# Retention and a squared-ReLU layer: flipping q and k two chunks ahead, with ScalarE's copies spread over a visit

## The chip, the cores and the metric

The kernel runs on one core of a Trainium2 chip. The metric is the device time of one execution in microseconds (us). The core's engines are TensorE (PE; its weight loads are listed as PEld), VectorE (DVE), ScalarE (ACT), GpSimd (POOL) and SyncE (SP), which here only issues transfers. Each works through its own queue of instructions in order, and they wait for each other by semaphores. SBUF is the on-chip memory of 128 partitions, PSUM the accumulators that matmuls write into.

## What is computed

```python
# q, k, v: (8 batches, 8 heads, 576 positions, 64), float32
scores = scale * np.matmul(q, k.transpose(0, 1, 3, 2))
Dmat = np.where(rel >= 0, gamma[:, None, None] ** rel[None, :, :], 0.0)   # decay by distance, causal
ret = np.matmul(scores * Dmat[None], v)
x = ret.transpose(0, 2, 1, 3).reshape(4608, 512)
h = np.maximum(x @ w_in, 0.0)          # w_in (512, 2048)
out = (h * h @ w_out).astype(np.float32)  # w_out (2048, 512)
```

The two weights come in double precision; the kernel turns them into float32 on the core. All matmuls are float32.

## The kernel before

The retention is done chunk by chunk: each batch's 576 positions are four chunks of 128 and one of 64, 40 chunks in all. The decay is split into a factor on q and one on v, so that a chunk needs only a causal mask; what earlier chunks contribute comes from a running 64x64 state per head (`u`). The first product (x @ w_in) follows in blocks of 512 tokens, by a Strassen-like scheme of seven products per tile, one product per "step"; its result goes to DRAM. The second product (L893) is a phase of its own behind all this.

One pass of the main loop is called a visit here. Visit i works on the retention of chunk i-1, makes the scores of chunk i, and does matmul steps of the first product (`ffn`) in two halves, as many as a schedule of tokens asks for: typically three or four per half, but one or two in the first half behind a chunk of 64.

From chunk 9 on, q and k are transposed on VectorE in 32x32 blocks (`flip`), and ScalarE puts the blocks where they belong with 16 small copies (8 for a chunk of 64), which are queued in `moves`:

```python
def scale_q(i, engine):                      # q times its decay factor
    ...
    engine.tensor_tensor(t, t, dv[...].to_broadcast([cs, H, D]), op=ALU.mult)              # L373

def new_qk(i):
    t = work2.tile([128, 2, HP, C], F32, tag="qk", name="qk")                              # two buffers
    ...
def flip(i):
    t = st[i]["flip"] = work2.tile([128, 4, 2, HP, 32], F32, tag="flip", name="flip")
    for j in (1, 0):                                                                        # k, then q
        nc.vector.transpose(t[:cs, :, j, :, :], loaded[i][j][:cs].rearrange(...))          # L390

def spread(i):
    to = new_qk(i)
    for b in range(chunks[i][3] // 32):
        for g in range(4):
            moves.append(lambda b=b, g=g: nc.scalar.copy(                                  # L396
                to[32 * g:32 * g + 32, :, :, 32 * b:32 * b + 32], st[i]["flip"][32 * b:32 * b + 32, g, :, :, :]))

def scores(i):
    ... nc.tensor.matmul(sc[e][rows(h), hp, :], lhsT=kT[...], rhs=qT[...], ...)            # L433, sc_ps
    ... nc.vector.tensor_tensor(r[:cs], both[:cs], msk[...], op=ALU.mult)                  # L441, mask; r lies in kT
    ... nc.gpsimd.tensor_tensor(vs[:cs], vs[:cs], dv[...], op=ALU.mult)                    # L443, decay of v

def retain_a(i):   # second half of the chunk with itself, state grows; nothing for a chunk of 64
    ... matmuls L455 (x_ps) and L458 (u_ps);  nc.scalar.copy(u_sb[...], u_ps[0])           # L464

def retain_b(i):   # what the state contributes
    ... nc.tensor.matmul(x_at(hp, b, h), lhsT=u[...], rhs=s["qT"][...], ...)               # L490, x_ps
    nc.scalar.copy(u_sb[...][:, 0:2, 0:1], xp[0][:, :, cs - CH:cs - CH + 1])               # L493, two numbers a row

def retain_c(i):   # first half of the chunk with itself (L455, L458), then
    ... nc.scalar.copy(xT[n][...], p[...])                                                  # L512
```

A step of the first product and its evacuation (`ffn_in`): eight matmul records of one tile (L614, h_a, h_b or h_c), then by the product's number

```python
if j == 0:   nc.scalar.copy(p1, p)                                  # L624, needed before product 3
elif j == 1: nc.vector.tensor_tensor(u2, p, p1, op=ALU.add)         # L626
elif j == 2: nc.vector.tensor_tensor(p15, p, p1, op=ALU.add)        # L628
elif j == 3: nc.scalar.activation(g["A11"], p, AF.Relu); ...        # L630, and a square on GpSimd, L631
elif j == 4: ... # L633, and a square on VectorE, L621
elif j == 5: ... # L637, L621
else:        ... # L640, L621
# then VectorE's sums of g (L552 to L555), of x (L538 to L541), and one piece of the
# conversion of w_out: L207, L211 and L215/L216 on ScalarE, L219, L222, L225, L242 to L245
```

The loop from chunk 5 on:

```python
def move(count):
    for f in moves[:count]:
        f()
    del moves[:count]
# ffn(i, half): for each of its steps: move(3); step()

else:
    ...
    if i + 1 < N_CH:
        scale_q(i + 1, nc.gpsimd)
    retain_a(i - 1)
    if i < N_TURN:                 # N_TURN = 9: chunks 0 to 8 are transposed on TensorE
        turn(i)
    ffn(i - 1, 0)
    move(len(moves))
    if N_TURN <= i + 1 < N_CH:
        flip(i + 1)
    retain_b(i - 1)
    if i < N_CH:
        scores(i)
    retain_c(i - 1)
    if N_TURN <= i + 1 < N_CH:
        spread(i + 1)
    ffn(i - 1, 1)
...
if i + 3 < N_CH:
    load(i + 3)                    # q, k and v of chunk i + 3
```

Of the kernel before, what the change touches and what calls it, by code (L numbers as in the profile page):

```python
# [9 lines left out]
F32 = mybir.dt.float32  # L10
# [5 lines left out]
C = 128  # L16
# [24 lines left out]
def kernel(  # L41
# [33 lines left out]
    nc = tc.nc  # L75
    ctx.enter_context(tc.manual_schedule())

    B, H, S, D = q.shape
    HP = H // 2
# [12 lines left out]
    N_CH = len(chunks)  # L92
# [6 lines left out]
    only = first.enter_context(tc.tile_pool(name="only", bufs=1))  # L99
    ld3 = first.enter_context(tc.tile_pool(name="ld3", bufs=3))  # L100
    ld4 = first.enter_context(tc.tile_pool(name="ld4", bufs=4))
    work = first.enter_context(tc.tile_pool(name="work", bufs=1))
    work2 = first.enter_context(tc.tile_pool(name="work2", bufs=2))
    ps_x = first.enter_context(tc.tile_pool(name="ps_x", bufs=1, space=PS))
    ps_t = first.enter_context(tc.tile_pool(name="ps_t", bufs=1, space=PS))
# [22 lines left out]
    loaded = {}  # L128
    N_EARLY = TOK // C

    def load(i):
        b, ci, c0, cs = chunks[i]
        got = {name: pool.tile([128, H, D], F32, tag=name, name=f"{name}_ld") for name, pool in (("q", ld3), ("k", ld4), ("v", ld4))}
        if i == 0:
            nc.sync.dma_start(dv, decays)
        for name, src in (("q", q), ("k", k), ("v", v)):
            t = got[name]

            issue = nc.scalar if i == 0 and name != "q" else nc.sync
            at = src[b, :, c0:c0 + cs, :].rearrange("h s d -> s h d")  # L140
            if name == "v":
                issue.dma_start(t[:cs], at)
            else:

                issue.dma_start(t[:cs, 0:H // 2, :], at[:, 0:H // 2, :])
                for e in range(2):
                    issue.dma_start(t[:cs, H // 2 + e::2, :], at[:, H // 2 + 1 - e::2, :])
        loaded[i] = [got["q"], got["k"], got["v"]]

# [166 lines left out]
    dv = only.tile([128, H, 2 * NCH], F32, name="dv")  # L318
    exp_bias = const.tile([128, 1], F32, name="exp_bias")
    nc.gpsimd.memset(exp_bias, -896.0 * 2.0 ** 23)  # L320
    idle = only.tile([128, 128], F32, name="idle")
    nc.vector.memset(idle, 1.0)
    load(0)
    load(1)
    fetch_raw(1)
    load(2)

    ident = only.tile([128, 128], F32, name="ident")
    make_identity(nc, ident)

    msk = only.tile([128, 1, 1, CH], F32, name="msk")
# [38 lines left out]
    def scale_q(i, engine):  # L370
        ci, cs = chunks[i][1], chunks[i][3]
        t = loaded[i][0][:cs]
        engine.tensor_tensor(t, t, dv[:cs, :, NCH + ci:NCH + ci + 1].to_broadcast([cs, H, D]), op=ALU.mult)  # L373
# [5 lines left out]
    moves = []  # L379

    def new_qk(i):
        t = work2.tile([128, 2, HP, C], F32, tag="qk", name="qk")
        st[i]["qT"], st[i]["kT"] = t[:, 0, :, :], t[:, 1, :, :]
        return t

    def flip(i):
        cs = chunks[i][3]
        t = st[i]["flip"] = work2.tile([128, 4, 2, HP, 32], F32, tag="flip", name="flip")
        for j in (1, 0):
            nc.vector.transpose(t[:cs, :, j, :, :], loaded[i][j][:cs].rearrange("s (p e) (d a) -> s (e d) p a", e=2, d=2))  # L390

    def spread(i):
        to = new_qk(i)
        for b in range(chunks[i][3] // 32):
            for g in range(4):
                moves.append(lambda b=b, g=g: nc.scalar.copy(  # L396
                    to[32 * g:32 * g + 32, :, :, 32 * b:32 * b + 32], st[i]["flip"][32 * b:32 * b + 32, g, :, :, :]))

    def move(count):
        for f in moves[:count]:  # L400
            f()
        del moves[:count]

    def turn(i):

        cs = chunks[i][3]
        n_h = cs // CH
        p = ps_t.tile([128, 2, 512], F32, tag="t", name="t_ps").rearrange("p h (j d t) -> p h j d t", j=2, d=HP)
        for j in (1, 0):
            for hp in range(HP):  # L410
                for h in range(n_h):
                    nc.tensor.transpose(p[:, h, j, hp, :], loaded[i][j][rows(h), 2 * hp:2 * hp + 2, :],
                                        ident[rows(h), rows(h)])
        to = new_qk(i)[:, :, :, :cs].rearrange("p j d (h t) -> p j d h t", h=n_h)
        nc.scalar.copy(to[:, 1].rearrange("p d h t -> p h d t"), p[:, :n_h, 1, :, :])
        nc.vector.tensor_copy(to[:, 0].rearrange("p d h t -> p h d t"), p[:, :n_h, 0, :, :])
# [78 lines left out]
    def retain_c(i):  # L495

        b_, ci, c0, cs = chunks[i]
        own, grow = within(i, 0)
        more = ci + 1 < NCH
        for j in range(0, len(own), 2):  # L500
            for f in own[j:j + 2] + (grow[j:j + 2] if more else []):
                f()
        tok = b_ * S + c0
        at = tok
        p = xp[0][:, :, 0:256].rearrange("p a (g t) -> p a g t", g=2)
        while at < tok + cs:
            n = at // TOK

            while steps and steps[0][0] <= (n - 2 if n > 4 else n - 3):
                step()  # L510
            end = min(tok + cs, (n + 1) * TOK)
            nc.scalar.copy(xT[n][:, :, at - n * TOK:end - n * TOK].rearrange("p (a g) t -> p a g t", a=2),  # L512
                           p[:, :, :, at - tok:end - tok])
            if more and at == tok:
                grown(i, 1)
            at = end
            if n_next[0] < N_BLK and (n_next[0] + 1) * TOK <= at:
                steps.extend(block_steps(n_next[0]))
                n_next[0] += 1
        st[i] = loaded[i] = None  # L520
# [175 lines left out]
    def ffn(i, half):  # L696

        gone[0] += chunks[max(0, min(i, N_CH - 1))][3] / 2
        if steps and steps[0][0] == 0:

            move(6)
            for f in (step, lambda: convert(6)) if half else (lambda: convert(6), step):
                f()
            if half and steps and steps[0][0] == 0:
                step()
                convert(6)
            return
        if not behind:
            behind.append((gone[0] - HALF, done[0]))
        points = behind + [p for p in PACE if p[0] > behind[0][0]]  # L710
        want = points[-1][1]
        for (x0, y0), (x1, y1) in zip(points, points[1:]):
            if gone[0] < x1:
                want = y0 + (y1 - y0) * (gone[0] - x0) / (x1 - x0)
                break
        count = max(1, int(want) - done[0])
        while steps and count:
            held[0] = half == 0 and count == 1
            move(3)
            step()  # L720
            count -= 1
        held[0] = False
# [15 lines left out]
    for i in range(N_CH + 1):  # L738
        if i <= N_EARLY:

            if i == 1:
                convert(2)
            elif i == 2:
                convert(5)
            if i >= 1:
                retain_a(i - 1)
                if i < 3:
                    warm(4, False)
                else:
                    convert(1)  # L750
                    first_in(2 * i - 5, (0,))
                    convert(5)
                retain_b(i - 1)
                if i < 3:
                    warm(4, False)
                retain_c(i - 1)
            convert((0, 1, 1, 0, 1)[i])
            if i == N_EARLY:
                fetch_raw(2)
                step()  # L760
            scores(i)
            if i == 2:
                convert(5)
                first_in(0, (0,))
            elif i == 3:
                convert(1)
                first_in(2, (0,))
                convert(5)
            elif i == N_EARLY:
                convert(5)  # L770
                step()
                convert(6)
            scale_q(i + 1, nc.gpsimd)
            if i < N_EARLY:
                if i < 2:
                    warm(6, False)
                turn(i + 1)
        else:
            if i == N_EARLY + 1:
                gone[0] = TOK  # L780
            if i + 1 < N_CH:
                scale_q(i + 1, nc.gpsimd)
            retain_a(i - 1)
            if i < N_TURN:
                turn(i)
            ffn(i - 1, 0)
            move(len(moves))
            if N_TURN <= i + 1 < N_CH:
                flip(i + 1)
            retain_b(i - 1)  # L790
            if i < N_CH:
                scores(i)
            retain_c(i - 1)
            if N_TURN <= i + 1 < N_CH:
                spread(i + 1)
            ffn(i - 1, 1)
        if i == 0:
            fetch_raw(2)
        if i + 3 < N_CH:
            load(i + 3)  # L800
        if 0 < i < N_EARLY:
            fetch_raw(1)
    assert n_next[0] == N_BLK
# [232 lines left out]
```

## Time and profile before

The kernel took 1007.21 us (median of three runs, 1002.46 to 1008.52); the profiled execution has a span of 1007.7 us.

| | busy us | share of the span |
|---|---|---|
| PE | 966.5 | 96% |
| PEld | 861.4 | 85% |
| DVE | 786.1 | 78% |
| ACT | 351.3 | 35% |
| POOL | 128.7 | 13% |

| operation | times | mean ns |
|---|---|---|
| flip of k, of q (L390, VectorE) | 31 each | 699, 664 (medians) |
| copy into qk (L396, ScalarE) | 440 | 402 |
| scale of q (L373, GpSimd) | 39 | 1210 |
| scores (L433, TensorE) | 1152 | 233 |
| matmuls of the first product (L614, h_b) | 736 | 387 |

How to read it: a busy share is an average over the whole span. The retention and the first product end at about 605 us, the rest is the second product. A line such as "PE sc_ps L433 <- ACT qk L396: 16.1, 19, 3.6" says that TensorE's matmuls of line 433 stood idle for 16.1 us in all, in 19 waits of at most 3.6 us, until ScalarE's instruction of line 396 released them. A group's line has its busy time and mean duration, then the idle time of the engine before it and what ended most of that. In a timeline a line has its start, its length, engine, line, operation, tiles and how many instructions were merged. Matmuls are pipelined, and their ends are modelled. The granted clock is the share of TensorE's full clock that the chip let through.

### The profile page before, as it was taken

The numbers are of one execution on the slowest core, as the hardware profiler recorded it, in microseconds if no ns is written. First come the engines' busy times: TensorE is split into PE (matmuls) and PEld (weight loads), VectorE is DVE, ScalarE is ACT, GpSimd is POOL, SyncE is SP. The second block draws the span as 40 slices with busy tenths as digits, with TensorE's granted clock in tenths as the row PEclk, the third lists the DMA queues.
The fourth block names the chain that finished last, engine by engine and source line by source line (L and its number), as shares of the span: only waits on it lengthen the run. The fifth ranks groups of instructions, "written<-read, shape, count | busy, mean of one in ns | idle before, by whom it ended". The sixth has DMA issues, their size and how long they took to land. (4 is left out here: it accounts for less than half of the span.)

```text
span 1007.7 us, 24117 instructions
## 1 busy us (share of the span) xinstructions
PE 966.5 (96%) x10092; PEld 861.4 (85%) x10092; DVE 786.1 (78%) x1458; ACT 351.3 (35%) x871; POOL 128.7 (13%) x121
## 2 busy tenths in 40 slices
PE   7899989999999899989989999999999999999998
PEld 6645768788878778877878889999999999999998
DVE  3789787768998799998977677777777677777766
ACT  3454575674665656746562110000000000000000
POOL 3211212312123131212120000000000000000000
PEclk7999999999999899999989999999999999999999
DMA  8883657655798589669437998684865757565351
GB/s 196 239 226 115 171 163 208 180 154 178 204 296 236 147 247 268 211 180 297 135 126 299 394 419 320 250 293 144 287 210 187 272 176 255 187 241 209 127 210 43
DMA packets 185037, 219.19 MB, mean 218 GB/s; under 512 B 118624, under 2 KB 135008, under 8 KB 175968
## 3 DMA queue, kind: packets, MB, share of 16 engines
q1 hardware_dynamic: 182816, 217.13, 66.3%
q8 instruction: 79, 1.29, 0.5%
q10 hardware_dynamic: 2112, 0.52, 0.2%
q14 instruction: 30, 0.25, 0.1%
HBM read 128.23 MB, written 89.39 MB: 216 GB/s over the span
## 5 line engine op out<-in xcount | busy, mean ns | idle before, releaser
L396 ACT COPY qk<-flip 32x256 f32<-32x256 f32 x440 | 177.1, 402 | 34.2 <-DVE flip L390 27.8
L614 PE MATMUL h_b<-room,w 128*128 128x256 f32 x736 | 179.4, 387 | 1.9 <-DVE room L539 1.6
L614 PEld LDWEIGHTS h_b<-room,w 128*128 128x128 f32 x736 | 139.6, 193 | 23.3 <-issue 2.1
L893 PE MATMUL o_b<-w,room 128*128 128x128 f32 x1168 | 144.5, 275 | 1.5 <-DVE room L844 1.5
L893 PEld LDWEIGHTS o_b<-w,room 128*128 128x128 f32 x1168 | 137.2, 192 | 1.7 <-DVE room L844 1.7
L893 PE MATMUL o_c<-w,room 128*128 128x128 f32 x1008 | 123.0, 275 | 0.0
L893 PEld LDWEIGHTS o_c<-w,room 128*128 128x128 f32 x1008 | 117.7, 192 | 0.0
L614 PE MATMUL h_c<-room,w 128*128 128x256 f32 x480 | 116.6, 386 | 0.0
L614 PE MATMUL h_a<-room,w 128*128 128x256 f32 x448 | 109.8, 389 | 3.1 <-ACT room L624 3.1
L907 ACT COPY r<-o_a 128x128 f32<-128x128 f32 x53 | 14.1, 265 | 273.3 <-PE o_a L893 242.5
L614 PEld LDWEIGHTS h_c<-room,w 128*128 128x128 f32 x480 | 91.8, 193 | 13.2
L614 PEld LDWEIGHTS h_a<-room,w 128*128 128x128 f32 x448 | 84.9, 193 | 15.7 <-ACT room L624 3.5
L893 PE MATMUL o_a<-w,a 128*128 128x128 f32 x688 | 85.6, 275 | 0.0
L631 POOL TENSOR_TENSOR room<-room 128x512 f32<-128x512 f32 x32 | 35.4, 1105 | 387.9 <-ACT room L630 368.5
L893 PEld LDWEIGHTS o_a<-w,a 128*128 128x128 f32 x688 | 81.2, 192 | 0.1
L621 DVE SCALAR_TENSOR_TENSOR room<-room 128x512 f32<-128x512 f32 x96 | 75.5, 786 | 3.3
L578 PE MATMUL h_ps<-room,w 128*128 128x512 f32 (+1 forms) x160 | 58.7, 515 | 3.5 <-DVE w L225 2.6
L373 POOL TENSOR_TENSOR q_ld<-q_ld,dv 128x512 f32<-128x512 f32 (+1 forms) x39 | 47.2, 1210 | 76.5 <-DMA q_ld<-in_q_dram 70.1
L455 PEld LDWEIGHTS x_ps<-qk,v_ld 64*64 64x64 f32 x1152 | 42.0, 141 | 15.3 <-issue 13.7
L433 PE MATMUL sc_ps<-qk 64*64 64x64 f32 x1152 | 35.5, 233 | 19.5 <-ACT qk L396 16.1
L455 PE MATMUL x_ps<-qk,v_ld 64*64 64x64 f32 x1152 | 51.1, 230 | 3.0 <-DVE qk L441 2.0
L633 DVE TENSOR_TENSOR room<-h_b,room 128x512 f32<-128x512 f32 x32 | 22.1, 690 | 39.0 <-PE h_b L614 38.9
(111 smaller groups left out, 1419.8 us busy)
## 6 DMA issues: line engine op xcount, KB each, us to landing
g_dram<-room SPq DMA_DIRECT2D x32, 1792.0 KB, 7.8
a<-g_dram SPq DMA_DIRECT2D x43, 1024.0 KB, 7.3
room<-g_dram SPq DMA_DIRECT2D x20, 1024.0 KB, 6.3
w<-w_dram SPq DMA_DIRECT2D x7, 1792.0 KB, 12.9
out_dram<-room SPq DMA_DIRECT2D x17, 512.0 KB, 3.3
w<-in_moe_w_in_dram SPq DMA_DIRECT2D x16, 512.0 KB, 5.7
w<-in_moe_w_out_dram SPq DMA_DIRECT2D x16, 512.0 KB, 3.8
v_ld<-in_v_dram SPq DMA_DIRECT2D x31, 256.0 KB, 4.0
```

Source lines behind the costliest of these rows:

```text
L373: engine.tensor_tensor(t, t, dv[:cs, :, NCH + ci:NCH + ci + 1].to_broadcast([cs, H, D]), op=ALU.mult)
L396: moves.append(lambda b=b, g=g: nc.scalar.copy(to[32 * g:32 * g + 32, :, :, 32 * b:32 * b + 32], st[i]["flip"][32 * b:32 * b + 32, g, :, : ...
L433: nc.tensor.matmul(sc[e][rows(h), hp, :], lhsT=kT[rows(e), hp, t], rhs=qT[rows(e), hp, t], start=True, stop=True, skip_group_check=True)
L455: own.append(lambda hp=hp, e=e, b=b: nc.tensor.matmul(x_at(hp, b, h), lhsT=s["vs"][rows(h), 2 * hp + b, :], rhs=s["ret"][rows(h), e, hp, : ...
L578: nc.tensor.matmul(p.rearrange("p h t -> p (h t)"), lhsT=w[:, c, :], rhs=xT[0][:, c, lo * HT:hi * HT], start=(c == 0), stop=(c == N_DM - 1))
L614: nc.tensor.matmul(p[:, mm, :], lhsT=w[:, c, :], rhs=xs[n][right][:, c, :], start=(j in OPENS and mm == 0 and c == 0), stop=(j in CLOSES a ...
L621: nc.vector.scalar_tensor_tensor(t, t, 0.0, t, op0=ALU.max, op1=ALU.mult)
L631: nc.gpsimd.tensor_tensor(g["A11"], g["A11"], g["A11"], op=ALU.mult)
L633: nc.vector.tensor_tensor(g["A22"], p, p15, op=ALU.add)
L893: nc.tensor.matmul(p, lhsT=s["lefts"][left][:, m, :], rhs=w_out[j][:, m, WO_SLOT[right], :], start=(i in OPENS and m == 0), stop=(i in CLO ...
L907: nc.scalar.copy(r[:, 0, 0:128], p)
```

## The change

q and k are loaded one chunk further ahead (v is not), with five buffers for k. q is scaled by GpSimd behind the scores, two chunks ahead, and both are flipped at the end of a visit, two chunks ahead. The copies of a chunk into its qk tile are queued with the flip, so that they spread over all steps of the next visit, three before each step; what is left of them when their own chunk's visit begins is done behind retain_a, before its first step. Since the qk tiles of three chunks are then alive, they have three buffers. Two small constant tiles move into a part of a weight's room that is free in this phase, which makes space. The purpose is that the scores of a chunk find their operands ready.

```diff
--- before.py
+++ after.py
@@ -99,7 +99,9 @@
     only = first.enter_context(tc.tile_pool(name="only", bufs=1))
     ld3 = first.enter_context(tc.tile_pool(name="ld3", bufs=3))
     ld4 = first.enter_context(tc.tile_pool(name="ld4", bufs=4))
+    ld5 = first.enter_context(tc.tile_pool(name="ld5", bufs=5))
     work = first.enter_context(tc.tile_pool(name="work", bufs=1))
+    work3 = first.enter_context(tc.tile_pool(name="work3", bufs=3))
     work2 = first.enter_context(tc.tile_pool(name="work2", bufs=2))
     ps_x = first.enter_context(tc.tile_pool(name="ps_x", bufs=1, space=PS))
     ps_t = first.enter_context(tc.tile_pool(name="ps_t", bufs=1, space=PS))
@@ -128,13 +130,15 @@
     loaded = {}
     N_EARLY = TOK // C
 
-    def load(i):
+    def load(i, names="qkv"):
         b, ci, c0, cs = chunks[i]
-        got = {name: pool.tile([128, H, D], F32, tag=name, name=f"{name}_ld") for name, pool in (("q", ld3), ("k", ld4), ("v", ld4))}
         if i == 0:
             nc.sync.dma_start(dv, decays)
-        for name, src in (("q", q), ("k", k), ("v", v)):
-            t = got[name]
+        got = loaded.setdefault(i, [None] * 3)
+        for name, pool, src in (("q", ld3, q), ("k", ld5, k), ("v", ld4, v)):
+            if name not in names:
+                continue
+            t = got["qkv".index(name)] = pool.tile([128, H, D], F32, tag=name, name=f"{name}_ld")
 
             issue = nc.scalar if i == 0 and name != "q" else nc.sync
             at = src[b, :, c0:c0 + cs, :].rearrange("h s d -> s h d")
@@ -145,7 +149,6 @@
                 issue.dma_start(t[:cs, 0:H // 2, :], at[:, 0:H // 2, :])
                 for e in range(2):
                     issue.dma_start(t[:cs, H // 2 + e::2, :], at[:, H // 2 + 1 - e::2, :])
-        loaded[i] = [got["q"], got["k"], got["v"]]
 
 
 
@@ -318,14 +321,13 @@
     dv = only.tile([128, H, 2 * NCH], F32, name="dv")
     exp_bias = const.tile([128, 1], F32, name="exp_bias")
     nc.gpsimd.memset(exp_bias, -896.0 * 2.0 ** 23)
-    idle = only.tile([128, 128], F32, name="idle")
+    idle, ident = (W[6][:, at:at + 128] for at in (2688, 2816))
     nc.vector.memset(idle, 1.0)
     load(0)
     load(1)
     fetch_raw(1)
     load(2)
 
-    ident = only.tile([128, 128], F32, name="ident")
     make_identity(nc, ident)
 
     msk = only.tile([128, 1, 1, CH], F32, name="msk")
@@ -379,7 +381,7 @@
     moves = []
 
     def new_qk(i):
-        t = work2.tile([128, 2, HP, C], F32, tag="qk", name="qk")
+        t = work3.tile([128, 2, HP, C], F32, tag="qk", name="qk")
         st[i]["qT"], st[i]["kT"] = t[:, 0, :, :], t[:, 1, :, :]
         return t
 
@@ -389,17 +391,16 @@
         for j in (1, 0):
             nc.vector.transpose(t[:cs, :, j, :, :], loaded[i][j][:cs].rearrange("s (p e) (d a) -> s (e d) p a", e=2, d=2))
 
-    def spread(i):
         to = new_qk(i)
-        for b in range(chunks[i][3] // 32):
+        for b in range(cs // 32):
             for g in range(4):
-                moves.append(lambda b=b, g=g: nc.scalar.copy(
-                    to[32 * g:32 * g + 32, :, :, 32 * b:32 * b + 32], st[i]["flip"][32 * b:32 * b + 32, g, :, :, :]))
-
-    def move(count):
-        for f in moves[:count]:
-            f()
-        del moves[:count]
+                moves.append((i, to[32 * g:32 * g + 32, :, :, 32 * b:32 * b + 32], t[32 * b:32 * b + 32, g, :, :, :]))
+
+    def move(count, i=N_CH):
+
+        while moves and count and moves[0][0] <= i:
+            nc.scalar.copy(*moves.pop(0)[1:])
+            count -= 1
 
     def turn(i):
 
@@ -778,26 +779,31 @@
         else:
             if i == N_EARLY + 1:
                 gone[0] = TOK
-            if i + 1 < N_CH:
-                scale_q(i + 1, nc.gpsimd)
             retain_a(i - 1)
             if i < N_TURN:
                 turn(i)
+            move(C, i)
             ffn(i - 1, 0)
-            move(len(moves))
-            if N_TURN <= i + 1 < N_CH:
-                flip(i + 1)
             retain_b(i - 1)
             if i < N_CH:
                 scores(i)
+            for j in range(i + 1 + (i > N_EARLY + 1), min(i + 3, N_CH)):
+                scale_q(j, nc.gpsimd)
             retain_c(i - 1)
-            if N_TURN <= i + 1 < N_CH:
-                spread(i + 1)
             ffn(i - 1, 1)
+            if N_TURN <= i + 2 < N_CH:
+                flip(i + 2)
         if i == 0:
             fetch_raw(2)
-        if i + 3 < N_CH:
+        if i < N_TURN - 1:
             load(i + 3)
+        else:
+            if i == N_TURN - 1:
+                load(i + 3, "qk")
+            if i + 4 < N_CH:
+                load(i + 4, "qk")
+            if i + 3 < N_CH:
+                load(i + 3, "v")
         if 0 < i < N_EARLY:
             fetch_raw(1)
     assert n_next[0] == N_BLK
```

## The prediction

> **What bounds the kernel now.** I read the windows first (busy time by stretch), then the waits of the first 560 us, then the timeline around single waits. After about 605 us only the second matrix product runs: TensorE is busy for 354.35 of the last 357 us, and the change touches nothing there. So everything has to be decided between 95 us (first flip) and 560 us. The columns are stretch, length, then busy time of PE, PEld, DVE, ACT, POOL, granted clock, DMA share, GB/s:
>
> ```profile
> 100.00:250.00 150.00, 143.41 (x1714) 118.89 (x1713) 116.33 (x178) 89.90 (x219) 36.97 (x32) 0.99 0.62 178
> 250.00:345.00 95.00, 89.56 (x1009) 75.56 (x1010) 83.81 (x137) 62.17 (x148) 21.12 (x19) 0.96 0.77 225
> 345.00:440.00 95.00, 89.50 (x1082) 75.10 (x1074) 90.14 (x143) 59.60 (x144) 20.86 (x18) 0.99 0.70 209
> 440.00:560.00 120.00, 113.51 (x1206) 96.28 (x1201) 96.09 (x157) 57.29 (x137) 23.28 (x21) 0.95 0.70 229
> ```
>
> TensorE bounds all four, but it is idle for 24.0 of 460 us (6.6 + 5.4 + 5.5 + 6.5), and VectorE is close behind it: 90.14 of 95 us in the third. The waits from 95 to 560 us say what ends the idle time (sum, times, longest):
>
> ```profile
> ACT qk L396 <- DVE flip L390: 27.8, 15, 5.7
> ...
> PE sc_ps L433 <- ACT qk L396: 16.1, 19, 3.6
> ...
> PE h_a L614 <- ACT room L624: 3.1, 1, 3.1
> ...
> PE x_ps L455 <- DVE qk L441: 2.0, 1, 2.0
> ```
>
> The scores wait for ScalarE's copies out of the flipped tile (16.1 us), and those had waited for VectorE's flips (27.8 us). The single wait of h_a has the same root: ScalarE's queue stood before a flip. The page gives the size of the copies:
>
> ```profile
> L396 ACT COPY qk<-flip 32x256 f32<-32x256 f32 x440 | 177.1, 402 | 34.2 <-DVE flip L390 27.8
> ```
>
> One such wait, in the timeline:
>
> ```profile
> 325.85 4.15 ACT L396 COPY qk<-flip 32x256 f32<-32x256 f32 x10
> ...
> 329.22 0.47 PE L433 MATMUL sc_ps<-qk 64*64 64x64 f32 x2 [2.17 <-ACT qk L396]
> ...
> 330.02 0.16 ACT L493 COPY u_sb<-x_ps 128x2 f32<-128x2 f32 x1
> ```
>
> Ten copies stand in a row because the first half-visit had only one matmul step to put them beside. The tiny copy L493 reads x_ps, which was finished at 326.79, and runs only behind the ten copies. It matters below: the next matmuls into x_ps (L455, retain_c) wait for L493, and in the timeline they start right after it wherever it comes late (330.19 and, after the last scores, 330.76 here).
>
> An idle TensorE costs twice. In the answer for 328.8 to 335.6 us the granted clock is
>
> ```profile
> 328.80:335.60 6.80, 6.02 (x53) 4.99 (x54) 5.30 (x8) 2.93 (x9) 0.58 (x1) 0.50 0.13 21
> ```
>
> and the eight h_a matmuls at 331.76 take 3.78 us instead of 1.89. In windows of 5 us there are five such dips after 100 us (at 135-145, 325-340, 435-445, 475-480 and 505-515), each after 2.1 us or more of idle time. Five times the sum of the missing clock is 12 us; about 1 us of it is idle anyway, so some 11 us are lost to slow matmuls.
>
> [...]
>
> **The change part by part.** Loads: q and k four chunks ahead. From 200 to 560 us GpSimd waited only 4.6 us for q, and the matmuls for no load at all; worth nothing by itself, it only makes the rest legal. Scaling: one 1.06 us operation moves a half-visit and a chunk; GpSimd is busy 13%, worth 0. Flips: the same 62 (0.70 and 0.66 us), moved from before retain_b to the very end of the visit, a chunk earlier. The mask product L441 thus no longer stands behind 1.37 us of flips, which should take about 1.4 of the 2.0 us that x_ps waited. Copies: the same 440 of 0.41 us, now three before each step of the whole following visit, and any rest right after retain_a. The scores of a chunk then find their copies done at least half a visit earlier.
>
> Removed idle time: 16.1 + 3.1 + 1.4 = 20.6 us. With the 11 us of clock the most that can be gained is 31.6 us, which would make 976 us.
>
> Added: the flips now come right before the copies that need them. ScalarE's first copy in a visit stops its queue until VectorE has worked off what it is behind and flipped. Before, that stop lay behind retain_c, with a whole visit until the next thing that TensorE needed of the queue's end. Now L493 comes half a visit after it. How far VectorE is behind at a visit's end can be read off. Start of retain_a and last VectorE operation of the steps before it:
>
> ```profile
> 311.62 0.27 PE L455 MATMUL x_ps<-qk,v_ld 64*64 64x64 f32 x2
> ...
> 312.29 0.68 DVE L640 TENSOR_TENSOR room<-h_b,room 128x512 f32<-128x512 f32 x1
> ...
> 314.21 0.68 DVE L222 TENSOR_TENSOR w<-w,w 128x512 f32<-128x512 f32 x1
> ```
>
> L222 ends at 314.89, 3.3 us after TensorE went on. Flips there end at 3.3 + 1.37 = 4.6. Then ScalarE has nine copies (3.7) for the three steps of this half, L624 (0.6) and L493 (0.16): done 9.1 us after the start. TensorE needs it after 0.65 (retain_a) + 3 x 1.79 + 1.43 (retain_b, scores, issue) = 7.45. So retain_c should wait 1.6 us in a visit that had no wait. I did the same for every visit from 119.7 us on, taking up to 1.37 us off the lag where VectorE had no idle time since the old flips. After a chunk of 64 there is no retain_a, and one or two steps leave 3.2 or 5.0 us only. The lags at 119.7, 186.3, 254.1, 324.5, 395.6 and 469.4 us were 3.7, 1.8, 3.6, 3.7, 3.4 and 1.3, and the waits come out at 3.2, 1.3, 2.5, 2.6, 2.9 and 0.5: 13 us. Full chunks: 1.9 (128.8), 1.5 (173.4), 1.9 (237.8), 1.3 (297.0), 1.6 (311.6), 0.8 (337.3), 1.0 (351.1), 1.5 (366.0), 2.1 (480.7) and 4.1 (497.0), 17.7 us, and 2 us in all others: 33 us. A wait of TensorE lets VectorE catch up, so these are not independent where VectorE is full; I choose three quarters, 25 us. Some six are long enough (over 2.1 us) for the clock to fall, about as many as now: 10 us lost there, as against 11.
>
> Sum: 1007 - 20.6 - 11 + 25 + 10 = 1010 us.
>
> **Rivals.** First, ScalarE's queue has more slack than I count (a lag much shorter because the flips no longer sit in mid-visit): the ceiling shrinks only by VectorE's limit, and the time is 976 to 988. For it: the visits at 193.9 to 223.1 us have lags of only 1.2 to 1.4. Against: from 237.8 us on, the conversion of the second weight adds about 0.7 us of VectorE work to every step. Second, VectorE becomes the bound: its 90.14 us in the third stretch leave at most 4.9 us of the 7 that are idle or slow there; in the others it has room. That alone would give about 985. Third, the waits on L493 don't thin each other out, and each of some 20 visits waits 2 us with two more drops of the clock: 1025 to 1035. Fourth, loads come too late or too early: the third stretch moves 209 GB/s and no matmul waits for them, so no change of time.
>
> **Range and chances.** Gain and cost are both near 30 to 35 us and rest on the same queue. I put the gain certain to about 4 us, the cost to about 15, so 8 in 10 lie between 988 and 1030. A gain of over 20 us needs the cost, idle time and clock together, to be below 12 instead of 35: 0.13. Over 20 us slower needs it above 50: 0.15. The rest, 0.72, is within 2%.
>
> **What would show it.** In the profile after, the wait of sc_ps for qk falls below 3 us (if not, the copies aren't early enough); a wait of x_ps L455 for ScalarE's L493, 0.9 us now, rises to 15 to 35 us (if it stays below 5, my cost is wrong and the time is below 990); the copies still wait for flips, over 25 us; the clock has four to seven dips between 100 and 560 us; the second product keeps its length. A wait for q or k loads, or for GpSimd, would be a cause that I haven't counted.

## The result and the profile after

The changed kernel takes 1047.03 us (median of four runs, 1044.28 to 1050.92) against 1007.5 us: a ratio of 1.041, with a 95% interval of 1.036 to 1.046. It is slower by 40 us. The predicted 1010 us (988 to 1030) was too low, and the result lies outside the range. What follows is read from the profiled execution, whose span is 1044.0 us. Line numbers have moved: the copies are L402 (were L396), the flips L392 (L390), the scores L434 (L433), retain_c's matmuls into x_ps L456 (L455), and the tiny copy out of x_ps is L494 (L493).

The waits of the kernel after (who waited, for whom: us in all, times, longest):

```profile
ACT qk L402 <- DVE flip L392: 72.0, 24, 7.0
...
PE x_ps L456 <- ACT u_sb L494: 49.3, 26, 4.6
```

The wait that the change was made against, sc_ps for the copies, is gone from TensorE's list. In its place x_ps waits for L494: 49.3 us, where the kernel before had 0.9:

```profile
PE x_ps L455 <- ACT u_sb L493: 0.9, 3, 0.4
```

And the copies, the same 440 of 403 ns, now wait 72.0 us for flips instead of 27.8:

```profile
L402 ACT COPY qk<-flip 32x256 f32<-32x256 f32 x440 | 177.1, 403 | 78.0 <-DVE flip L392 72.0
```

The visit that the prediction worked out (it began at 311.62 us before) begins at 333.47 us after. First VectorE, then ScalarE, then TensorE in the timeline of the kernel after:

```profile
337.11 0.68 DVE L225 TENSOR_TENSOR w<-w,w 128x512 f32<-128x512 f32 x1
...
337.71 0.70 DVE L392 STREAM_TRANSPOSE flip<-k_ld 128x512 f32<-128x512 f32 x1
338.34 0.67 DVE L392 STREAM_TRANSPOSE flip<-q_ld 128x512 f32<-128x512 f32 x1
```

```profile
334.24 0.37 ACT L465 COPY u_sb<-u_ps 128x256 f32<-128x256 f32 x1 [3.85 <-PE u_ps L459]
339.05 1.24 ACT L402 COPY qk<-flip 32x256 f32<-32x256 f32 x3 [4.43 <-DVE flip L392]
340.31 0.59 ACT L625 COPY room<-h_a 128x512 f32<-128x512 f32 x1
340.92 2.47 ACT L402 COPY qk<-flip 32x256 f32<-32x256 f32 x6
343.30 0.15 ACT L494 COPY u_sb<-x_ps 128x2 f32<-128x2 f32 x1
```

```profile
339.99 0.65 PE L434 MATMUL sc_ps<-qk 64*64 64x64 f32 x16
343.50 0.37 PE L456 MATMUL x_ps<-qk,v_ld 64*64 64x64 f32 x2 [2.86 <-ACT u_sb L494]
```

VectorE comes to the flips 4.2 us after TensorE has begun the visit. ScalarE stands still for 4.43 us, then does nine copies and one evacuation, and only then, in the order of its queue, L494, which was ready at about 340.2 and starts at 343.30. TensorE waits 2.86 us in a place where it had not waited at all.

The clock adds to it. These are the sums over the half-speed stretches from 95 to 640 us, five before and ten after:

```profile
sum 23.90, PE 21.63 PEld 17.65 DVE 14.00 ACT 15.53 POOL 6.55; mean PE 4.33 PEld 3.53 DVE 2.80 ACT 3.11 POOL 1.31
```

```profile
sum 40.90, PE 38.30 PEld 30.93 DVE 16.48 ACT 24.66 POOL 11.06; mean PE 3.83 PEld 3.09 DVE 1.65 ACT 2.47 POOL 1.11
```

The granted clock in them is 0.50: the eight h_b matmuls from 203.49 us after take 3.67 us, where eight h_a of the same shape from 198.44 us, at full clock, take 1.89. So half of TensorE's busy time in the stretches is counted as lost: 10.8 us before, 19.2 us after. The page of the kernel after has TensorE's busy time:

```profile
PE 973.1 (93%) x10092; PEld 864.2 (83%) x10092; DVE 784.1 (75%) x1458; ACT 350.8 (34%) x871; POOL 126.2 (12%) x121
```

So the 36.3 us between the two spans are 29.7 us of idle TensorE (70.9 us now, 41.2 before) and 6.6 us of longer busy time. The clock's part of the latter is 3.5 us: the 8.4 us between 10.8 and 19.2, less 4.9 us that the kernel before lost in a further half-speed stretch from 8.0 to 18.2 us (9.86 us of busy TensorE), before the first flip, where the other profile has none. The other 3.1 us stay unnamed. The idle part adds up from the waits: L494 +48.4, scores -16.1, h_a -2.7, the mask product L441 -2.0, evacuations by VectorE about +3.

### The profile page after: what moved, and what is told of

Same layout as the page of the kernel before. It is cut to its first block, busy times and chain, and to the rows that moved or that the text cites. A ratio compares the mean times of both kernels' runs of the same rounds, so it can differ in the third digit from the quotient of the medians.

```text
span 1044.0 us, 24095 instructions
## 1 busy us (share of the span) xinstructions
PE 973.1 (93%) x10092; PEld 864.2 (83%) x10092; DVE 784.1 (75%) x1458; ACT 350.8 (34%) x871; POOL 126.2 (12%) x121
## 5 line engine op out<-in xcount | busy, mean ns | idle before, releaser
L402 ACT COPY qk<-flip 32x256 f32<-32x256 f32 x440 | 177.1, 403 | 78.0 <-DVE flip L392 72.0
L615 PE MATMUL h_b<-room,w 128*128 128x256 f32 x736 | 182.2, 391 | 4.8 <-DVE room L634 3.1
L615 PE MATMUL h_c<-room,w 128*128 128x256 f32 x480 | 119.8, 394 | 0.0
L615 PE MATMUL h_a<-room,w 128*128 128x256 f32 x448 | 111.9, 394 | 0.4 <-ACT room L625 0.4
L615 PEld LDWEIGHTS h_c<-room,w 128*128 128x128 f32 x480 | 93.9, 197 | 14.0
L456 PE MATMUL x_ps<-qk,v_ld 64*64 64x64 f32 x1152 | 51.9, 233 | 49.3 <-ACT u_sb L494 49.3
L456 PEld LDWEIGHTS x_ps<-qk,v_ld 64*64 64x64 f32 x1152 | 42.1, 142 | 64.3 <-ACT u_sb L494 35.3
L622 DVE SCALAR_TENSOR_TENSOR room<-room 128x512 f32<-128x512 f32 x96 | 72.4, 754 | 3.3
L579 PEld LDWEIGHTS h_ps<-room,w 128*128 128x128 f32 x160 | 29.2, 190 | 25.3 <-issue 22.1
## 6 DMA issues: line engine op xcount, KB each, us to landing
w<-w_dram SPq DMA_DIRECT2D x7, 1792.0 KB, 12.1
```

The lines of the kernel that those rows point to most:

```text
L402: nc.scalar.copy(*moves.pop(0)[1:])
L456: own.append(lambda hp=hp, e=e, b=b: nc.tensor.matmul(x_at(hp, b, h), lhsT=s["vs"][rows(h), 2 * hp + b, :], rhs=s["ret"][rows(h), e, hp, : ...
L579: nc.tensor.matmul(p.rearrange("p h t -> p (h t)"), lhsT=w[:, c, :], rhs=xT[0][:, c, lo * HT:hi * HT], start=(c == 0), stop=(c == N_DM - 1))
L615: nc.tensor.matmul(p[:, mm, :], lhsT=w[:, c, :], rhs=xs[n][right][:, c, :], start=(j in OPENS and mm == 0 and c == 0), stop=(j in CLOSES a ...
L622: nc.vector.scalar_tensor_tensor(t, t, 0.0, t, op0=ALU.max, op1=ALU.mult)
```

## The experiments

Theory A: the flips are given to VectorE too late. ScalarE's first copy in a visit stops the queue, and L494 stands in it. Theory B: nine to twelve copies in the first half are too many for ScalarE in front of L494, whether it has to wait for flips or not. Theory C: the flips at the visit's end hold up VectorE's evacuations, and L494 only shows it. L494 orders retain_c's matmuls into x_ps behind retain_b's; no run leaves it out.

All of these are changes to the changed kernel, apart from the loads alone. The kernel before ran beside each (1007.3 us).

**The flips half a visit earlier, before retain_b (e3).** Their copies still begin in the next visit; q is scaled at the visit's start instead of behind the scores.

```diff
+            scale_q(...)                      # at the visit's start, as before
             retain_a(i - 1)
             ...
             ffn(i - 1, 0)
+            flip(i + 2)                       # its copies are held back to the visit's end
             retain_b(i - 1)
             ...
             ffn(i - 1, 1)
-            flip(i + 2)
```

> The changed kernel with the flips of chunk i+2 given to VectorE half a visit earlier, before retain_b, as in the kernel before (and q scaled at the visit's start for that); their copies still begin in the next visit, three before each step. Theory A, ScalarE stops at the first copy because VectorE was given the flips only just before, and L494 stands behind: the copies' wait for flips falls from 72 us to under 15, the wait of x_ps for L494 from 49 us to under 10, the clock has at most 4 half-speed stretches between 100 and 600 us instead of 10, and the time is 980 to 1000 us. Theory B, nine to twelve copies in the first half are too many for ScalarE whether it waits or not: the wait for L494 stays over 25 us and the time over 1025 us.

Measured: 1001.01 us, ratio 0.994 (0.992 to 0.996). The copies don't wait for flips any more, and there are two half-speed stretches. TensorE's waits from 95 to 620 us of this kernel:

```profile
PE x_ps L456 <- ACT u_sb L494: 14.0, 11, 2.9
PE x_ps L456 <- DVE qk L442: 3.9, 3, 2.0
```

The same visit as above, ScalarE's timeline:

```profile
311.03 1.23 ACT L402 COPY qk<-flip 32x256 f32<-32x256 f32 x3
312.65 0.59 ACT L625 COPY room<-h_a 128x512 f32<-128x512 f32 x1 [0.39 <-PE h_a L615]
313.26 2.48 ACT L402 COPY qk<-flip 32x256 f32<-32x256 f32 x6
316.76 0.16 ACT L494 COPY u_sb<-x_ps 128x2 f32<-128x2 f32 x1 [1.02 <-PE x_ps L491]
```

The same nine copies now end 1 us before the matmuls (L491) whose result L494 reads. That is theory A: 35 of the 49 us come from the flips' lateness. But 14 us stay, more than the 10 that A allowed, and the time is 1 us above its range. So B has a share.

**No copies before the first half's steps; flips left where the change has them.**

```diff
-            move(3)
+            if half:
+                move(3)
             step()
```

> The changed kernel with no copies before the steps of a visit's first half: they are done before the steps of its second half and, for the rest, behind retain_a of the next visit. Flips stay at the visit's end. Theories A and B agree: nothing that waits for a flip stands before L494, its wait falls under 5 us and the time is 980 to 1000 us. Theory C, the late flips hold up VectorE's evacuations of the first half and L494 only shows it: TensorE's waits move to VectorE lines, over 25 us in sum, and the time stays over 1025 us.

Measured: 1002.46 us, ratio 0.995 (0.992 to 0.998). TensorE's waits from 95 to 620 us:

```profile
PE h_b L615 <- DVE room L634: 7.8, 6, 3.1
PE x_ps L456 <- ACT u_sb L494: 7.1, 6, 2.1
PE sc_ps L434 <- ACT qk L402: 3.2, 4, 1.5
```

This falls just outside the expected range, and the wait for L494 is 7.1 us instead of under 5. Four half-speed stretches are left after 95 us, 17.2 us in all; the profile is of the slowest of the ten runs, 1007.48 us. The two longest waits for L494, 2.1 us each, show what else stands before L494. ScalarE's timeline of this kernel for both:

```profile
250.29 0.72 ACT L218 ACTIVATE w<-w,exp_bias 128x512 uint32<-128x512 uint32 x1 [2.90 <-DVE w L210]
...
251.47 0.14 ACT L494 COPY u_sb<-x_ps 128x2 f32<-128x2 f32 x1
```

```profile
498.96 5.41 ACT L402 COPY qk<-flip 32x256 f32<-32x256 f32 x13
505.37 0.72 ACT L218 ACTIVATE w<-w,exp_bias 128x512 uint32<-128x512 uint32 x1 [1.01 <-DVE w L210]
```

ScalarE's part of the weight's conversion (L218, then L219) waits for VectorE's part L210, as it does in the kernel before too (8.3 us in all there, 11.4 here). In the other case thirteen copies are left over from a visit with a single step in its second half. VectorE's evacuations hold TensorE up for 8 us, not for 25: theory C isn't the cause of the 49 us. Whether the late flips cause these 8 us stays open, as the fastest kernel below, whose flips come in mid-visit, has 6.7 us of the same wait.

**One copy instead of three before each step of the first half.**

```diff
-            move(3)
+            move(3 if half else 1)
             step()
```

> The changed kernel with one copy instead of three before each step of a visit's first half (the second half keeps three); flips stay at the visit's end. Theory A takes the wait in front of L494 as flip wait plus copies: two copies fewer a step take 0.82 us times the number of steps of the half off each visit's wait, which leaves about 14 us of the 49 (10 to 20), at visits with one or two steps mostly, and 1000 to 1015 us. If only the flip counted and not the copies behind it, the wait would stay above 35 us and the time above 1030 us.

Measured: 1010.43 us, ratio 1.003 (1.002 to 1.004). From 95 to 620 us:

```profile
ACT qk L402 <- DVE flip L392: 51.4, 23, 5.3
PE x_ps L456 <- ACT u_sb L494: 20.7, 14, 3.0
```

The time is in the expected range, the wait for L494 just above it. Subtracting 0.82 us a step from each wait gave 14; the size is half as large again, because three of the waits (2.68, 3.02 and 2.85 us, at 126, 404 and 506 us) follow a short half of one or two steps, where there are few copies to take away, or left-over copies, and one (2.72 us at 248 us) is the conversion's wait for VectorE again. Still, 28 us went with the copies (48.8 us in the same stretch of the changed kernel): the wait is flip plus copies, in a chain.

**Each flip of k done twice.** The second does the same work over again; 0.70 us more of VectorE before the copies of each chunk.

```diff
-        for j in (1, 0):
+        for j in (1, 1, 0):
             nc.vector.transpose(...)
```

> The changed kernel with each flip of k done twice (0.70 us more VectorE time in front of the copies, 31 times, 22 us of VectorE time in all). Theory A: each of some 24 waits for L494 grows by about 0.7 us, in sum from 49 to 62 to 70 us, and with the clock the time grows by 15 to 25 us to about 1065. Theory B: the waits grow by under 5 us, and so does the time.

Measured, one run: 1074.57 us. From 95 to 620 us:

```profile
ACT qk L402 <- DVE flip L392: 91.3, 27, 7.7
...
PE x_ps L456 <- ACT u_sb L494: 58.8, 26, 5.4
```

The direction is A's, the split isn't: the wait for L494 stays under 62 us, and the time goes over 1065. The copies wait 19 us longer, which is nearly the 22 us of VectorE time put in, but the matmuls wait only 10 us longer (48.8 in the same stretch of the changed kernel). That VectorE catches up while TensorE waits would explain the half that is missing; it isn't tested apart. The two spans differ by 28.8 us. Besides the 10, 11.6 go to the clock after 95 us (fourteen half-speed stretches with 61.6 us of busy TensorE, half of it lost, against 19.2 us), 2.3 to waits for L625, and 6.1 to three half-speed stretches before 95 us (12.1 us busy), ahead of the first flip, where the changed kernel's profile has none. These 6 us can't come from the doubled flips; without them the growth is about 22 us, within A's 15 to 25.

**L494 done by VectorE.**

```diff
-        nc.scalar.copy(u_sb[...][:, 0:2, 0:1], xp[0][:, :, cs - CH:cs - CH + 1])
+        nc.vector.tensor_copy(u_sb[...][:, 0:2, 0:1], xp[0][:, :, cs - CH:cs - CH + 1])
```

> The changed kernel with the tiny copy L494 (out of x_ps, two numbers a row) done by VectorE instead of ScalarE, all else alike. Theories A and B: the wait of x_ps for ScalarE is gone, and x_ps waits for VectorE's lag in mid-visit instead, 1 to 2 us in some 15 visits: 10 to 30 us in sum, time 1005 to 1035 us. Theory C: no change, 1040 to 1050 us.

Measured, one run: 1087.21 us, the slowest of all. From 95 to 620 us:

```profile
ACT qk L402 <- DVE flip L392: 69.1, 24, 7.0
...
PE x_ps L456 <- DVE u_sb L494: 67.3, 27, 5.6
```

Wrong for every theory as to size. The wait follows the queue that L494 is put in, as A and B say, and C is out. The edit also acts before 95 us, where the chunks aren't flipped yet: over the whole run the wait is 80.2 us. But VectorE is further behind in mid-visit than 1 to 2 us: flips, evacuations and the conversion of the weight all stand before it there.

**The loads alone.** The kernel before with q and k loaded a chunk further ahead, and the buffers for it.

```diff
-        for name, src in (("q", q), ("k", k), ("v", v)):
+        for name, pool, src in (("q", ld3, q), ("k", ld5, k), ("v", ld4, v)):
...
-            load(i + 3)
+            load(i + 4, "qk")
+            load(i + 3, "v")
```

> The kernel before with nothing but the loads of q and k a chunk further ahead, five buffers for k, three for qk and the two constants in the weight's room; scaling, flips and copies stay where they were. All theories: 1003 to 1011 us, ratio within half a per cent of 1, and the waits of sc_ps for copies stay at about 16 us.

Measured: 1008.26 us, ratio 1.000 (0.999 to 1.001). The wait of the scores (L435 in this kernel, for the copies L398) stays, as expected:

```profile
PE sc_ps L435 <- ACT qk L398: 16.6, 19, 3.6
```

Loads and buffers neither cost nor bring anything.

**Flips behind the mask product (e7).** As in the first experiment, but given to VectorE after the scores' mask product instead of before retain_b.

```diff
+            scale_q(...)                      # at the visit's start, as in e3
             ...
             scores(i)
+            flip(i + 2)                       # its copies are held back to the visit's end
             retain_c(i - 1)
             ffn(i - 1, 1)
-            flip(i + 2)
```

> As the kernel with the flips in mid-visit (e3), but given to VectorE behind the mask product of the scores instead of in front of it; copies still in the next visit, three before each step of both halves. Theory A: the wait of x_ps for the mask (3.9 us there) falls under 2 us, the wait for L494 stays about 14 us, and the time is 996 to 1001 us. If the flips' place against the mask doesn't matter, 1001 us and the mask's wait stays.

Measured: 997.57 us, ratio 0.991 (0.987 to 0.994). From 95 to 620 us:

```profile
PE x_ps L456 <- ACT u_sb L494: 15.7, 11, 3.0
...
PE x_ps L456 <- DVE qk L442: 1.2, 2, 0.8
```

The wait for the mask product is 1.2 us instead of 3.9, that for L494 15.7 us, both as expected. A gain in time over e3 isn't shown: the two intervals overlap, and both profiled executions have a span of 995.2 us.

**And all copies in the second half of the following visit.**

```diff
-            move(6)                           # another branch of ffn, with its own steps
+            if half:
+                move(6)
...
-            move(3)
+            if half:
+                move(4)
             step()
...
-            move(C, i)
             ffn(i - 1, 0)
...
             ffn(i - 1, 1)
+            move(C)                           # what is left of the chunk's copies
```

> As e7, but all copies of a chunk are done in the second half of the visit behind its flips (four before each step, the rest at the visit's end), so that nothing that waits for a flip and no copy at all stands before L494. Theory A: the wait for L494 falls under 3 us, that of sc_ps for copies stays under 3 us, at most 3 half-speed stretches after 100 us, and the time is 985 to 996 us. Rival: sixteen copies in three steps hold up L625 and L631 on ScalarE, TensorE waits for those over 10 us, and the time is over 1000 us.

Measured: 990.75 us, ratio 0.983 (0.979 to 0.987): faster than the kernel before by 1.7% and than the changed one by 56 us. One half-speed stretch is left between 95 and 640 us. TensorE's waits from 95 to 620 us:

```profile
PE h_b L615 <- DVE room L634: 6.7, 6, 2.5
PE h_b L615 <- DVE room L540: 2.5, 2, 1.6
PE x_ps L456 <- ACT u_sb L494: 2.4, 3, 1.6
PE sc_ps L434 <- ACT qk L402: 1.7, 2, 1.1
```

With the copies out of the first half, 2.4 us of the wait for L494 are left, and the scores wait only 1.7 us for their operands. The rival's fear, copies that hold up L625 and L631, doesn't come true: no matmul waits for either. Most of what remains of the idle time is VectorE's.

## Why the prediction was wrong

**What is removed: right.** Predicted were 16.1 us for the scores, 3.1 for h_a and 1.4 for the mask product, 20.6 us in all. The waits fell by 16.1, 2.7 and 2.0, 20.8 us. Loads and scaling were put at nothing; the loads alone measured 1.000. The scaling wasn't moved alone, but no matmul of the profile after waits for GpSimd.

**The mechanism of what is added: right.** "L493 comes half a visit after it" is what the trace and the experiments show: the wait falls to 14.0 us when the flips come earlier, to 7.1 us when the copies leave the first half's steps, and to 2.4 us with both and no left-over copies in front. Four signs hold too: the scores' wait is gone, the copies wait over 25 us for flips, no load stops TensorE, and the second product keeps its length (from its first matmul, at 608.35 us before and 644.81 us after, to the end it takes 399.3 and 399.2 us). Two signs don't hold: the wait for L494 is 49 us, above the 15 to 35, and there are ten dips of the clock, not four to seven. One reading of the lines was wrong: in the profile before no matmul of L455 starts at 330.19 us. The first starts at 330.76, behind the scores, so that place doesn't show L455 held up by L493; the profile after does, at 343.50.

**The size of what is added: wrong, and this is the term that failed.** The sum had 25 us; the wait for L494 rose by 48.4 us. Two steps of it are mis-sized.

First, "I choose three quarters, 25 us": the visits' sum was 33 us, and even it was 15 us short. It missed four things. The lag at a visit's end was reduced by up to 1.37 us because the flips had left the middle of the visit, which by the prediction's rule makes about 2.1 us on average over the 21 visits of full chunks from 151.9 to 533.4 us of the profile after; measured there, it is 2.6 us, nearly the 2.7 us that the same visits had before. That VectorE's lag builds up again in the visit's second half would explain it; this isn't tested. In the worked visit it is even 4.2 us instead of 3.3. And the rest of a chunk's copies, which comes behind retain_a, wasn't counted at all. It matters in the visit that follows one with a short first half. At 362.9 us of the profile after no copy waits for a flip any more, and ScalarE is busy without a break:

```profile
364.02 4.15 ACT L402 COPY qk<-flip 32x256 f32<-32x256 f32 x10
368.19 0.72 ACT L218 ACTIVATE w<-w,exp_bias 128x512 uint32<-128x512 uint32 x1
368.81 0.67 ACT L219 ACTIVATE w<-w 128x512 f32<-128x512 uint32 x1
369.51 1.23 ACT L402 COPY qk<-flip 32x256 f32<-32x256 f32 x3
370.77 0.60 ACT L631 ACTIVATE room<-h_a 128x512 f32<-128x512 f32 x1
371.39 1.23 ACT L402 COPY qk<-flip 32x256 f32<-32x256 f32 x3
```

That visit waited 2.94 us where 0.8 were estimated, and the six that follow a short first half waited 10.9 us where the prediction lists 4.8 (1.9, 0.8 and 2.1). The six visits with the short half themselves were nearly right: 16.2 us for 13. Of the 14.0 us that e3 kept, 8.2 are in the six. The conversion pair L218 and L219, 1.3 us here, isn't in the worked sum, nor is its own wait for VectorE. Last, the first visit that is touched (1.9 us, at 97 us) had been left out.

Second, the factor of three quarters itself. Of 0.70 us put in by the doubled flip, about half came out as wait, so waits may make each other smaller. But the lags were read from a trace in which TensorE also waited, and the effect may have been in them already and been taken off twice. That is argued, not shown; measured is only that the waits came to more than the unscaled sum.

**The clock: wrong by 9 us.** "Some six are long enough" became ten stretches and 19.2 us instead of 10. More waits passed 2.1 us than were estimated: nine of the ten stretches follow one. The tenth follows a wait of 1.7 us at 201.2 us, while waits of 2.8 us at 259.9 and 478.6 us had none behind them, so the length that I took for a threshold is none. In this trace it matters where a wait falls. The ten stretches begin at 128.41, 142.07, 189.85, 203.51, 278.60, 343.45, 357.11, 374.17, 435.61 and 544.84 us, whole multiples of 3.4133 us apart to within 0.01 us (142.07 - 128.41 is four of them, 544.84 - 128.41 is 122), and eight of them last one such length, two last two (6.83 us from 142.07 and 435.61 us). In windows of this length, laid from these times (columns as in the prediction), the wait of 1.7 us lies in a single one, the wait at 259.9 us in two:

```profile
200.09:203.51 3.42, 1.73 (x67) 1.39 (x65) 2.61 (x5) 2.57 (x7) 0.00 (x0) 1.00 0.26 58
203.51:206.92 3.41, 3.41 (x10) 2.50 (x8) 0.00 (x0) 1.58 (x4) 0.00 (x0) 0.50 0.44 99
258.12:261.53 3.41, 1.82 (x52) 1.32 (x50) 3.38 (x7) 3.33 (x8) 1.53 (x2) 1.00 0.51 189
261.53:264.95 3.42, 2.23 (x39) 1.99 (x40) 2.12 (x3) 2.55 (x8) 2.43 (x2) 1.00 0.93 347
```

TensorE is idle for 1.69 us of the first, and 1.59 and 1.19 us of the last two; the wait at 478.6 us leaves 1.36 and 1.49 us. From 95 to 640 us of this profile every window at full clock with 1.69 us or more of idle TensorE is followed by half clock, and none with 1.61 us or less. 1.69 us is about half of the 3.413 us of a window, but no sharp limit: in the kernel with all copies in the second half 1.44 us were followed by half clock (at 326.06 us), and 1.94 us (from 353.37 us) were not.

Together: 48.4 instead of 25, and 19.2 instead of 10. That is 33 us of the 34 between the 1010 predicted and the profiled span of 1044. That it fits so closely is in part chance. The kernel before lost 4.9 us of half clock before 18.2 us that the changed one didn't; the changed one has about 3 us more of waits for VectorE; and some 3 us stay unnamed.

**The rivals.** The third, that the waits don't thin each other out, is what happened, with 1025 to 1035 us named and the clock's part too small in it (two more dips, where there were five). The first pointed to the short lags near 200 us, and those stayed as they were (1.1 to 1.4 us from 207 to 236 us); but a visit there still waited when left-over copies came into it. The second, VectorE as the bound, shows only in the best version, whose largest remaining waits are VectorE's, at 990.75 us where the prediction had put about 985.

## What to carry to other kernels

When work is moved to spread it, look in the queue that it moves into for the next instruction that another engine waits for: here a copy of two numbers a row that orders matmuls cost 49 us because a wait, and the copies behind it, were put in front of it. A producer on a busy engine should be asked for its work at least as early as that engine is behind, and the consumer's queue should hold nothing urgent until then: earlier flips gave 0.6%, and together with copies that no urgent instruction stands behind 1.7%. An estimate made visit by visit found the mechanism and most of the places; the mistakes were to scale its sum by hand, to take the lag for shorter than it was, and to leave out the left-over work of the visits that follow a short one.

## What the runs showed of the hardware

A wait of TensorE of 1.7 us was followed by a stretch at half clock (at 201.2 us after the change; granted clock 0.50 from 203.51 us), while waits of 2.8 us (at 259.9 and 478.6 us) were not: the half-speed stretches of that profile begin on a grid of 3.413 us, and the first wait lay within one window of it (1.69 us idle), the others were split over two (at most 1.59 us idle in one). Moving the two-number copy L494 from ScalarE (median 0.16 us) to VectorE (0.15 us at 166.39 us) made the kernel 40 us slower in one run, and from 95 to 620 us the matmuls into x_ps waited 67.3 us for it instead of 48.8: its price is the queue it stands in.
